# A conditioned transformer block on one core: the prologue is reordered, the first attention block runs over two key halves, and its first denominators move to TensorE

## The chip, the core and the metric

The kernel runs on one core of a Trainium2 chip. The metric is the device time of one execution in microseconds (us). A core has TensorE (PE; its weight loads are listed as PEld), VectorE (DVE), ScalarE (ACT), GpSimd (POOL) and SyncE (SP), each with its own instruction stream; they meet at semaphores. SP issues nearly all DMAs here. Matrix products go to PSUM, which has 8 banks of 512 f32 columns on 128 partitions.

## The reference

```
mod = silu(c) @ w_mod              # 1024 -> 6 x 1024: sa, ca, ga, sb, cb, gb
h = layernorm(x) * (1 + ca) + sa   # x is 2048 x 1024, bf16
q = h @ wq (32 heads of 32);  k = h @ wk;  v = h @ wv     # one k and one v for all heads
p = softmax(q k^T / sqrt(32));  a = (p v) @ wo
x = x + ga * a
h = layernorm(x) * (1 + cb) + sb
x = x + gb * ((silu(h @ w1) * (h @ w3)) @ w2)             # F = 3584
```

`ca` is called the scale part of the modulation below, and `sa` the shift part.

## The kernel before, in words

**A planner writes the order.** `Dag.add` (line 42) records every operation with its engine, the keys it reads and writes, a planned duration and a priority (a lower number goes first). `Dag.schedule` (line 106) then plays the whole program through with these durations and fixes one order per engine; `emit` writes it with semaphore waits. So an engine executes in a fixed order, and an operation that waits holds up all that stands behind it on its engine. `clear` keys make an operation wait for earlier readers and writers; `after` fixes the order of DMAs on SP. On PE score products (class S) come first, value and denominator products (V, D) next to them, and all other products are filler by priority and by order in the program. For a product group the planner also picks a free PSUM bank. Line 205 has a rule that holds a long DVE operation back while a product group is about to end; with `LOOK = 0.0` (line 13) it is off.

**Prologue (lines 455 to 761).** SP loads the 16 tiles of x (128 x 1024) into 8 slots and the first 2048 columns of `w_mod` (shift and scale together) in 8 row blocks of 512 KB, in the order of the list `ORDER` (line 645). The condition vector goes through silu to `SCT`; 128 products with one moving column each (line 677) give shift and scale. DVE makes `MODC` (1 + scale, line 687) and `SAB` (shift, line 689). Each x tile gets its statistics (`ln_stats`, line 506, on DVE; two tiles by `ln_stats_act`, line 514, on ACT), its factor on POOL (`ln_scale`, line 528), and is normalised on DVE (`ln_norm`, line 542). `ln_transpose` (line 548) transposes it on PE against the identity (line 558) and ACT (line 569) or DVE (line 572) copies it to `HT`. Scale and shift are not applied to the tiles: the scale goes into the weights (`WQ`, `WKV`: lines 719, 721 and 750), the shift into biases (products of the raw weights with `SAB`, lines 693 to 708 and 741), which are added when K (`kproj`, line 603), V (`vproj`, line 616) and Q (`qproj`, line 627) leave PSUM (lines 612, 622, 632). Then `gate` (line 768) makes `ga` and `gb` on all partitions, with weights in three slots `WMS`; `ga` is multiplied into `WO` (line 794). Lines 809 and 817 make `cb` and `sb`. The Q products of the later 1536 rows (line 824) are filler of the first attention block.

**Attention (line 830), for each of 8 blocks of 256 queries.** A block loops over 8 groups of four heads (f) and 8 steps of 256 keys. A step has 8 score products of 32 x 256 (line 855, four of them side by side on the array's row quarters) and two exponentials of 128 x 1024 on ACT (line 865), which write slot u of 11 in `UREG`. DVE adds the exponentials of four steps into a tree tile `TR` (lines 879 and 884: per group 6 additions of 128 x 2048), and line 889 folds the group's two tree tiles into one, for groups 0 to 6. Value products (line 902) take the slots as moving operand; denominator products (line 922) multiply the folded tile with a selection matrix `SEL`, one group behind. DVE copies sums to `ASB` (line 929) and denominators to `DSB` (lines 937, 940), takes reciprocals (line 946), spreads them over the partitions (`stream_shuffle` into `RB`, line 952) and multiplies (line 957).

**After a block: `post` (line 982).** Products with `WO` (line 996), the residual, the second normalisation, transposes (on PE in the first and the last block, by DMA in the others), then the gated network in 14 pairs of groups (products line 1030, tanh on ACT line 1039, line 1042 and 1047 on DVE) and the last products (line 1064). Its products are filler under the next block's attention.

Of the kernel before, what the change touches and what calls it, by code (L numbers as in the profile page):

```python
# [8 lines left out]
P = 128  # L9
# [3 lines left out]
LOOK = 0.0  # L13
# [15 lines left out]
class Dag:  # L29


    def __init__(self, nc):
# [7 lines left out]
        self.chain = 0  # L40

# [64 lines left out]
    def schedule(self, banks):  # L106
# [41 lines left out]
        while left:  # L148
# [56 lines left out]
            if e == "dve" and LOOK and n.dur > 0.9 and n.prio > 1:  # L205
                fin = None
                for b in banks:
                    g = bank_group[b]
                    rem = [x for x in g.nodes if x.start is None and x.eng == "pe"] if g is not None else []
                    if rem:  # L210
                        f1 = t_free["pe"] + sum(x.dur for x in rem) + 0.26
                        if fin is None or f1 < fin:
                            fin = f1
                if fin is not None and t < fin < t + LOOK:
                    t_free["dve"] = fin
                    continue
            ready[e].remove(n)
# [132 lines left out]
def build(nc, x_in, wq_in, wk_in, wv_in, wo_in, w1_in, w3_in, w2_in, c_in, wmod_in, out, S, D, F):  # L350
# [34 lines left out]
    BP = (0, 0, 0)  # L385
    WP = (4, 4, 4)
    RP = (0, 0, 0)
# [6 lines left out]
    RB = sb("RB", [P, QB], F32)  # L394
    WKR = sb("WKR", [P, NC, 4, 32], BF16)
    ASB = XN[:, 2:4, :].rearrange("p a d -> p (a d)").bitcast(F32).rearrange("p (a q) -> p a q", a=4)
    DSB = WKR[:].rearrange("p c a f -> p (c a f)").bitcast(F32).rearrange("p (a q) -> p a q", a=2)
# [25 lines left out]
    NR = len(RING)  # L423
    assert NF * QB + 2 * 4096 <= NC * S and NXS == 8
# [5 lines left out]
    WQ0R = WKR[:].rearrange("p c a f -> p c (a f)")  # L430
    WQ0K = ["WKR"]
# [20 lines left out]

    cuts = {}
    G.add("pool", lambda e: e.memset(SEL[:], 0.0), writes=["SEL"], dur=0.3)
    for a, fs in enumerate(DGRP):
        edge = [32 * j // len(fs) for j in range(len(fs) + 1)]
        for j, f in enumerate(fs):
# [4 lines left out]
    G.add("pool", lambda e: e.memset(IDENT[:], 0.0), writes=["IDENT"], dur=0.2)  # L462
    G.add("pool", lambda e: e.affine_select(IDENT[:], IDENT[:], pattern=[[-1, P]], compare_op=ALU.not_equal,
                                            fill=1.0, base=0, channel_multiplier=1),
          reads=["IDENT"], writes=["IDENT"], dur=0.4)

# [5 lines left out]
    def xload(t0, n):  # L472
        r = []
        for t in range(t0, t0 + n):
            r.append(dma(lambda e, t=t: e.dma_start(X[:, t % NXS, :], x2[t * P:(t + 1) * P, :]),
                         ("x", t % NXS), writes=[("X", t % NXS)], nbytes=P * D * 2))
        return r

    WQK = [("WREG", "q")]
    xload(0, 8)  # L480

    def wmload(k, after=()):
# [52 lines left out]
    def xnt(q):  # L535

        return XN[:, q, :] if q < 4 else UREG[:, (NU + NTR - 2) * 2048 + (q - 4) * D:][:, 0:D]
# [607 lines left out]
```

## Time and profile before

| | us |
|---|---|
| median of 3 runs | 1168.52 (1167.83 to 1172.24) |
| the profiled execution, its own time | 1172.46 |
| its span | 1170.7 |
| PE busy | 1124.0 (96%) |
| ACT busy | 1028.9 (88%) |
| DVE busy | 1013.7 (87%) |
| exponentials (line 865), 1024 instructions | 974.3 |
| first exponential starts | 36.41 |
| DMA, of 211 MB in all | mean 180 GB/s; 397 to 404 GB/s from 5 to 20 us |

All durations in the prediction come from this one profiled execution, so its sums are made against 1170.7 us of span, and 1172.46 of time. Idle time is charged to what ended it. "PEclk" is the granted TensorE clock, 1.00 being full speed. In rows of a timeline the first number is the start, the second the time that the row takes. In rows of a window the first number after the borders is the window's length, and each engine's busy time is followed by its number of instructions.

### The profile page before, as it was taken

Reading aid. Unit: us, or ns where it says so; the run is one execution under the profiler, and the core shown is the slowest. Engines: PE = TensorE matmul, PEld = TensorE weight load, DVE = VectorE, ACT = ScalarE, POOL = GpSimd, SP = SyncE. Lnnn points to the kernel's source line nnn. Section 1 sums busy time; section 2 is a strip of 40 time slices with the busy share of each in tenths; the row PEclk is TensorE's granted clock in tenths of the full one; section 3 lists DMA queues with packets and bytes.
Section 4 is the critical chain, followed back from the end, with each engine's and each line's share of the span. In section 5 each row is a group of like instructions: output and inputs, shape, how many; then the busy total and the mean of one; then the engine's idle time right before and its main releaser. Section 6 shows DMA issues by size and latency. Waiting matters only on the chain.

```text
span 1170.7 us, 34975 instructions
## 1 busy us (share of the span) xinstructions
PE 1124.0 (96%) x15561; PEld 757.9 (65%) x15561; DVE 1013.7 (87%) x1504; ACT 1028.9 (88%) x1174; POOL 43.1 (4%) x86
## 2 busy tenths in 40 slices
PE   4898997999989999999999999999999999999998
PEld 4554442667656676676666766767666757677887
DVE  7687988898988999899989998999989998997451
ACT  3798999899999999999999999999999999992110
POOL 5100000000010001000000001000100000000000
PEclk9897998899999999999999999999999999999999
DMA  9606007365757565966587566856596658656996
GB/s 348 216 23 196 19 2 181 109 181 160 200 129 211 169 169 133 278 182 170 156 233 204 164 179 175 246 166 174 144 257 176 191 145 246 198 161 176 299 291 154
DMA packets 383222, 211.05 MB, mean 180 GB/s; under 512 B 21600, under 2 KB 374880, under 8 KB 383072
## 3 DMA queue, kind: packets, MB, share of 16 engines
q1 hardware_dynamic: 380992, 208.69, 63.4%
q8 instruction: 122, 2.00, 0.7%
q10 hardware_dynamic: 2080, 0.13, 0.1%
q14 instruction: 28, 0.23, 0.1%
HBM read 201.46 MB, written 4.19 MB: 176 GB/s over the span
## 4 chain that ended last, share of the span: by engine, by line
PE 74%; ACT 15%; DVE 8%; issue 2%; POOL 1%; DMA 0%; SPq 0%
PE PB L1030 23%; PE PB L1064 15%; ACT UREG L865 14%; PE SP L855 11%; PE PB L902 9%; PE PB L629 4%; PE PB L996 4%; PE SP L1030 3%; DVE UREG L884 2%; PE SP L1064 2%; DVE UREG L879 1%; PE PB L922 1%; PE PB L608 1%; DVE HREG L1042 1%; PE SP L558 1%
## 5 line engine op out<-in xcount | busy, mean ns | idle before, releaser
L865 ACT ACTIVATE UREG<-SP 128x1024 bf16<-128x1024 f32 x1024 | 974.3, 1113 | 21.1 <-PE SP L855 18.8
L884 DVE TENSOR_TENSOR UREG<-UREG 128x2048 bf16<-128x2048 bf16 x256 | 311.9, 1218 | 11.6 <-ACT UREG L865 9.4
L855 PE MATMUL SP<-QT,KT 32*128 32x256 bf16 x4096 | 206.4, 276 | 16.4 <-ACT UREG L865 15.8
L1030 PE MATMUL PB<-QT,WREG 128*128 128x256 bf16 x1632 | 205.6, 273 | 0.8 <-DVE WKR L940 0.4
L1030 PEld LDWEIGHTS PB<-QT,WREG 128*128 128x128 bf16 x1632 | 148.2, 98 | 47.1 <-issue 31.7
L879 DVE TENSOR_TENSOR UREG<-UREG 128x2048 bf16<-128x2048 bf16 x128 | 156.2, 1220 | 13.2 <-ACT UREG L865 9.6
L855 PEld LDWEIGHTS SP<-QT,KT 32*128 32x128 bf16 x4096 | 61.0, 92 | 141.0 <-ACT UREG L865 91.8
L902 PE MATMUL PB<-UREG,V 128*32 128x256 bf16 x4032 | 134.1, 282 | 1.4 <-ACT UREG L865 1.4
L1030 PE MATMUL PB<-QT,HREG 128*128 128x256 bf16 x1056 | 132.9, 273 | 0.7 <-DVE WKR L940 0.4
L902 PEld LDWEIGHTS PB<-UREG,V 128*32 128x32 bf16 x4032 | 101.2, 99 | 28.4 <-issue 17.5
L1030 PEld LDWEIGHTS PB<-QT,HREG 128*128 128x128 bf16 x1056 | 96.1, 98 | 29.7 <-issue 19.7
L1064 PE MATMUL PB<-WREG,HREG 128*128 128x256 bf16 x840 | 104.9, 273 | 0.5 <-DVE HREG L1042 0.5
L1064 PEld LDWEIGHTS PB<-WREG,HREG 128*128 128x128 bf16 x840 | 77.8, 98 | 22.2 <-issue 12.6
L1030 PE MATMUL PB<-QT,X 128*128 128x256 bf16 x544 | 69.1, 273 | 1.1 <-DVE WREG L1037 0.7
L629 PE MATMUL PB<-HREG,WREG 128*128 128x512 bf16 (+1 forms) x312 | 67.8, 355 | 1.8 <-ACT HREG L569 0.9
L889 DVE TENSOR_TENSOR UREG<-UREG 128x2048 bf16<-128x2048 bf16 x56 | 68.2, 1218 | 0.4
L1064 PE MATMUL PB<-HREG 128*128 128x256 bf16 x532 | 67.1, 273 | 0.0
L1039 ACT ACTIVATE GSB<-GSB 128x512 bf16<-128x512 bf16 x56 | 41.6, 742 | 28.1 <-DVE GSB L1037 28.1
L929 DVE COPY XN<-PB 128x256 f32<-128x256 f32 x63 | 26.6, 422 | 39.8 <-PE PB L922 38.0
L1039 ACT ACTIVATE WREG<-WREG 128x512 bf16<-128x512 bf16 x56 | 42.8, 765 | 20.1 <-DVE WREG L1037 20.1
L1030 PEld LDWEIGHTS PB<-QT,X 128*128 128x128 bf16 x544 | 49.8, 98 | 15.9 <-issue 10.7
L996 PE MATMUL PB<-WO,QT 128*128 128x512 bf16 x232 | 57.8, 381 | 0.4 <-DVE WREG L1070 0.4
(130 smaller groups left out, 1004.2 us busy)
## 6 DMA issues: line engine op xcount, KB each, us to landing
WREG<-in_B_w_dram SPq DMA_DIRECT2D x112, 512.0 KB, 5.1
HREG<-in_B_w_dram SPq DMA_DIRECT2D x74, 512.0 KB, 5.4
WREG<-in_B_w_dram SPq DMA_DIRECT2D x33, 896.0 KB, 5.2
X<-in_B_w_dram SPq DMA_DIRECT2D x38, 512.0 KB, 5.0
HREG<-in_B_w_dram SPq DMA_DIRECT2D x21, 896.0 KB, 5.3
X<-in_B_w_dram SPq DMA_DIRECT2D x10, 896.0 KB, 5.0
X<-in_A_x_dram SPq DMA_DIRECT2D x32, 256.0 KB, 5.6
WREG<-in_w_mod_dram SPq DMA_DIRECT2D x16, 512.0 KB, 5.2
```

What stands on the lines that cost most here:

```text
L629: g = mm_group(NC, lambda e, b, c: e.matmul(b[:, 0:n], WQ[:, c, f * P:(f + 1) * P], HT[:, c, sl], start=c == 0, stop=c == NC - 1), lambda ...
L855: r = e.matmul(SP[:, b, o:o + qn], KT[32 * gg:32 * gg + 32, kts[j] * P:(kts[j] + 1) * P], QT[32 * gg:32 * gg + 32, f, q0:q0 + qn], start=T ...
L865: G.add("act", lambda e, u=u, h0=h0, n=n, b0=b0, nb=nb: e.activation(U[:, u, h0 * W:(h0 + n) * W].rearrange("p (b w) -> p b w", b=nb), SP[ ...
L879: G.add("dve", lambda e, tr=tr, u=u, fu=first_u: e.tensor_tensor(TR[:, tr, 0:4 * W], U[:, fu, 0:4 * W], U[:, u, 0:4 * W], ALU.add), reads= ...
L884: G.add("dve", lambda e, tr=tr, u=u: e.tensor_tensor(TR[:, tr, 0:4 * W], TR[:, tr, 0:4 * W], U[:, u, 0:4 * W], ALU.add), reads=[("TR", tr) ...
L889: G.add("dve", lambda e, ta=ta, tb=tb: e.tensor_tensor(TR[:, ta, 0:4 * W], TR[:, ta, 0:4 * W], TR[:, tb, 0:4 * W], ALU.add), reads=[("TR", ...
L902: r = e.matmul(PB[g.bank][32 * gg:32 * gg + 32, 0:qn], V[:, kt, :], U[:, pu, (gg * npk + j) * qn:(gg * npk + j + 1) * qn], start=w0 + n == ...
L929: G.add("dve", lambda e, g=g, f=f: e.tensor_copy(ASB[:, f % 4, 0:qn], PB[g.bank][:, 0:qn]), writes=[("ASB", f % 4), ("XN", 2 + f % 4 // 2) ...
L996: g = mm_group(NC, lambda e, b, f, t=t, h=h: e.matmul(b, QT[:, f, t * P:(t + 1) * P], WO[:, f, h * 512:(h + 1) * 512], start=f == 0, stop= ...
L1030: return e.matmul(b[:, j * qn:(j + 1) * qn], w13[:, w, c, j * P:(j + 1) * P], QT[:, c, q0:q0 + qn], start=c == 0, stop=c == NC - 1)
L1039: G.add("act", lambda e, b=b: e.activation(TB[b], GS[b], ACT.Tanh, scale=0.5), reads=[("GS", b)], writes=[("TB", b)], clear=alias("TB") if ...
L1064: G.add("pe", lambda e, g=g, j=j, fc=fc, hf=hf, first=first, w2s=w2s: e.matmul(PB[g.bank][:, j * 256:(j + 1) * 256], HHT[:, hf * NH + fc, ...
```

## The change

Seven things, in the order of the program:

1. **The planner's hold on DVE** is rewritten and switched on. A DVE operation planned at over 0.9 us (tree sums and folds) is put off if an operation of priority -1 or less is ready within 0.5 us, or, if neither of PSUM banks 0 and 1 is idle or about to be, until the next product group ends, when that is within 0.6 us. It acts in all blocks.
2. **Dummy products** of 128 x 128 identity on PE can be planned into idle time up to `WARM`; with `WARM = 0.0` none are made.
3. **Loads.** The modulation is loaded in halves of 256 KB per row block: the scale half (`a`) of all rows is in front of the shift half (`s`). The raw `wq` goes to `WO`'s place in three cuts (group 0, groups 1 to 3, groups 4 to 7), and `wo` is loaded there once their readers are done.
4. **Scaling into new places.** Scaled K and V weights get their own tile `WKS`; scaled Q weights go from `WO` to `WQ`, so that products no longer wait for the bias products to have read the raw ones. Scaling of groups 1 to 3 is shared between ACT and DVE, that of groups 4 to 7 has the last priority on DVE. Biases come in three sets, each with its Q cut.
5. **Transposes.** All 16 normalised tiles get places of their own. A transpose group waits for all its tiles. Tiles 0 to 7 are evicted by ACT, tiles 8 to 15 by DVE.
6. **The first attention block** is split: groups 0 to 3 (`HEAD`) first run over keys 0 to 1023, then over keys 1024 to 2047, then groups 4 to 7 run as before. For the halves of groups 0 to 3 there are no tree sums: `DIRECT` has PE sum the exponentials themselves with `SEL`. The second half's sums are added to the first's in `ASB`.
7. **Priorities after the first block**: `BP` and `RP` become 5 for it (normalisation, transposes and division ahead of the rest of DVE). `RB` moves into the tile of normalised rows, with four slots in the first block: all spreads first, then all products.

The core of the diff:

```diff
-LOOK = 0.0
+LOOK = 0.5
+LK = 0.6
+LF = 0.5
+UP = -1
...
-            if e == "dve" and LOOK and n.dur > 0.9 and n.prio > 1:
...
+            if e == "dve" and n.dur > 0.9 and n.prio > UP:
+                soon = [c for c in cands if c[1].prio <= UP and c[0] < t + LOOK]
+                if soon:
+                    t_free[e] = min(c[0] for c in soon)
+                    continue
+                fin = t + LK
+                for b in (0, 1):
+                    i = bank_idle(b)
+                    if i is not None and i <= t + LF:
+                        fin = None
+                        break
...
-    BP = (0, 0, 0)
+    BP = (5, 0, 0)
...
-    RP = (0, 0, 0)
+    RP = (5, 0, 0)
+    RBQ = (0,)
...
+    WARM = 0.0
+    HEAD = 4
+    DIRECT = (0, 1)
...
-                G.add("pe", tr, reads=[("XN", q0 + i), "IDENT"] + xnk(q0 + i), dur=ncb * 0.065, lat=0.2,
+                G.add("pe", tr, reads=["IDENT"] + [k for j in (range(nt) if i == 0 else (i,)) for k in [("XN", q0 + j)] + xnk(q0 + j)], dur=ncb * 0.065, lat=0.2,
...
-    ONACT = (3, 6)
...
-    ORDER = ("w0", "w1", "w2", "w3", "x8", "x9", "w4", "x10", "x11", "w5", "w6", "w7", "q", "x12", "x13", "x14", "x15")
...
+    ONACT = (2, 5)
...
+    QACT = 1
+    TRP = 1
+    EV = (("act",), ("act",), ("dve",), ("dve",))
+    ORDER = ("x0", "x1", "x2", "x3", "x4", "x5", "a0", "a1", "x6", "a2", "a3", "x7", "a4", "a5", "a6", "a7", "q0",
+             "s0", "s1", "s2", "s3", "s4", "s5", "s6", "s7", "q1", "x8", "x9", "x10", "x11", "x12", "x13", "x14", "x15", "q2")
+    QCUT = (0, 1, HEAD, NC)
...
+    gm = [grp((0,)), grp((1,))]
+    for h in (1, 0):
+        for k in range(NC):
...
+    def wscale(a, keys):
+        G.add("dve", lambda e: e.tensor_tensor(WKS[:, a], WKV[:, a], bc1(32), ALU.mult), reads=[("MODC", 1)] + keys,
+              writes=[("WKS", a)], dur=dve_t(256), prio=-5 if a == 0 else 1)
...
+            if k == 1 and c % 2 < QACT:
+                G.add("act", lambda e, c=c: e.activation(WQ[:, c, a:b], WO[:, c, a:b], ACT.Identity, scale=MODC[:, 1, c:c + 1]),
+                      reads=[("MODC", 1), ("WQR", k)], writes=wr, dur=act_t(b - a), prio=1)
...
+    bias(0, (0,), kb=True)
+    G.chain = 0
+    kproj(0, 256, (2, 3, 4, 5, 6, 7))
+    qproj(0, 256, 0, (2, 3, 4, 5, 6, 7), prio=1)
+    kproj(256, 256, (2, 3, 4, 5, 6, 7))
+    kproj(512, 512, (1,))
+    wscale(1, WVK)
+    qscale(1)
+    bias(1, (0,), vb=True)
+    qproj(0, 256, 1, (0, 1))
+    vproj(0, (0, 1))
+    vproj(1, (0, 1))
+    for f in range(2, HEAD):
+        qproj(0, 256, f, (0, 1))
+    tr(8, 4, (0, 1))
...
+    bias(2, (0, 1))
+    G.chain = 0
+    qscale(2)
     wo_load = dma(lambda e: e.dma_start(WO[:], wo_in.rearrange("(c p) f -> p c f", p=P)), "wo", writes=["WO"],
...
+                  clear=[("WQR", k) for k in range(3)], nbytes=D * D * 2, after=xl)
...
+            direct = q0 == 0 and f < HEAD and s // per_t in DIRECT
...
+            if direct:
+                ds.append((f, pend, h))
+                dprev[0] = None
...
+                            a = U[:, a[0]] if us else TR[:, a]
...
+            if h == 1:
+                G.add("dve", lambda e, g=g, f=f: e.tensor_tensor(ASB[:, f % 4, 0:qn], ASB[:, f % 4, 0:qn], PB[g.bank][:, 0:qn], ALU.add),
...
+        if q0 == 0:
+            head = []
+            for h in range(2):
+                for f in range(HEAD):
+                    head += [(f, s) for s in range(h * per_t, (h + 1) * per_t)] + [(f, (h,))]
+            sched = head + [x for x in sched if x[0] >= HEAD]
...
+    G.warm = (WARM, P / 2400.0 + 0.0026, warm, ident)
```

## The prediction

> **What bounds the kernel now.** I read the page's busy slices first, to see which engines are full and when.
>
> ```profile
> PE   4898997999989999999999999999999999999998
> ACT  3798999899999999999999999999999999992110
> PEclk9897998899999999999999999999999999999999
> ```
>
> One slice is 29.3 us. PE and ACT are both full from the third slice on; the gaps are at the start, in slices 5 to 8, and on ACT at the end. Next I cut the span at every 128th exponential (128 exponentials are one block of 256 queries) and read busy time and clock per stretch. The columns are PE, weight load, DVE, ACT, POOL, granted clock, DMA.
>
> ```profile
> 0.00:36.40 36.40, 20.87 (x361) 17.43 (x365) 29.03 (x71) 14.72 (x26) 16.19 (x48) 1.00 1.00 353
> ...
> 36.40:171.50 135.10, 126.91 (x1773) 63.11 (x1767) 109.85 (x157) 124.46 (x136) 2.20 (x6) 0.91 0.25 79
> 171.50:300.00 128.50, 114.83 (x1642) 73.16 (x1635) 114.51 (x163) 123.15 (x141) 2.49 (x4) 0.93 0.55 152
> ...
> 426.13:552.26 126.13, 125.87 (x1803) 85.64 (x1801) 117.49 (x171) 125.47 (x143) 3.44 (x4) 1.00 0.69 190
> ```
>
> The repeating block takes 126.13 us with PE busy 125.87 and ACT 125.47: a new prologue has nothing to win there. What can be won lies in three stretches: the 36.4 us before the first exponential, block 0 (135.1), block 1 (128.5). The rest, 1170.7 - 300.0 = 870.7 us, I keep. On ACT, block 0 shows a hole:
>
> ```profile
> 45.76 2.37 ACT L569 ACTIVATE HREG<-PB 128x512 bf16<-128x512 bf16 x4
> 48.01 1.03 ACT L865 ACTIVATE UREG<-SP 128x1024 bf16<-128x1024 f32 x1
> 48.92 2.09 ACT L569 ACTIVATE HREG<-PB 128x512 bf16<-128x512 bf16 x4
> 50.83 1.09 ACT L865 ACTIVATE UREG<-SP 128x1024 bf16<-128x1024 f32 x1
> 56.38 3.77 ACT L865 ACTIVATE UREG<-SP 128x1024 bf16<-128x1024 f32 x4 [4.46 <-PE SP L855]
> ```
>
> From 45.8 to 56.4 ACT does two exponentials. It evicts the last 8 transposed pieces (4.5 us) and then waits 4.46 us for scores, because keys 1536 to 2047 are late. Last, the DVE timeline from modulation to first scores:
>
> ```profile
> 26.02 0.11 DVE L687 TENSOR_SCALAR MODC<-PB 128x8 f32<-128x8 f32 x1
> ...
> 26.24 1.22 DVE L721 TENSOR_TENSOR WREG<-WKR,MODC 128x1024 bf16<-128x1024 bf16 x1
> ...
> 29.69 0.15 DVE L711 COPY BIA<-PB 128x2 f32<-128x2 f32 x1
> ...
> 34.86 0.48 DVE L632 TENSOR_SCALAR QT<-SP,BIA 128x256 bf16<-128x256 f32 x1 [0.53 <-PE SP L629]
> ```
>
> The modulation is there at 26.1, yet the first exponential runs at 36.41. These 10.3 us hold the weight scaling, the bias copy behind normalisations on DVE, a K product (1.90 us) and a Q product, with transposes between.
>
> **Start: 36.4 becomes 25.5.** The new order loads 8 x tiles, 8 scale halves, the first Q columns, then 8 shift halves. Scale and shift are each 2.1 MB. Bytes against time come from the modulation products of before: the fourth weight row (4.3 MB with x) was there at 15.1 us, and the fifth (5.4 MB) at 17.7, after a DMA wait. So scale is complete near 15.1. Shift is complete at 6.7 MB, 1.3 MB past 17.7 us, at 340 to 400 GB/s: 21.0 to 21.6, I take 21.3. Now K and Q products no longer wait for shift; only their evictions do, through the bias. So the chain after 21.3 is: last modulation product and semaphores 0.5, SAB copy 0.4, bias products for Q and K 0.8 (their rows now are 0.40 and 0.38), copy 0.3, KT and QT evictions 0.48 each, scores to exponential 0.6: 3.6 us, plus 0.6 for a DVE instruction in the way. That is 25.5. Scale first thus does not start anything by itself: the shift part ends the wait as before, but 6 us of other work has moved ahead of it. Bounds: 24 with DVE free, 30 if the chain stretches to 8 us, near its present 10.3.
>
> The SP queue issues all of this without a wait (26 issues of about 0.45 us, row median of w_mod, done by 12.5 us), and tile 8 is the first that waits for a slot. The Q columns in 256 KB took 9.9 us to land at the end of the queue; now they delay shift by their bytes, counted above. The two small POOL fills of IDENT move ahead of SEL: nothing waits for SEL until the denominators.
>
> **Block 0: 135.1 becomes 128.** Four query groups run over keys 0 to 1023 first: 4 x 8 = 32 exponentials at 0.92 us (20 in 18.45 us in the chain) give 29 us of work, from 25.5 to about 55, before the second key half is wanted. Its x tiles land by about 28 and need 8 x 2.1 us of DVE (two statistics 1.28, aggregate 0.20, normalise 0.55) and 16 evictions of 0.41, 23 us together; DVE has room because the tree sums of these groups are gone. So the hole closes: 4.46 us of wait off. The 8 evictions leave ACT: 4.4 off. Scaling Q weights on ACT adds 4 x 0.45 = 1.8. That gives 135.1 - 4.5 - 4.4 + 1.8 = 128.0.
>
> DIRECT sums denominators on PE: per group 64 column tiles in each of two halves against 8 after the fold, a row of 4 tiles taking 0.116 us (64 in 1.86). Per half 8 rows of 4, so 64 rows for 4 groups, less 8: 56 x 0.116 = 6.5 us more PE. It saves DVE 4 x 7 x 1.22 = 34.2 us, and adds 8 evictions, 3.4 us. DVE was busy 109.85 of 135.1, so its saving alone is worth nothing after about 60 us. PE is where it tells: 126.9 + 6.5 = 133.4 us does not fit into 128. What makes room is the clock: it was 0.91 on the mean, and 0.50 from 44.5 to 55, in the hole, where about 9 us busy cost 4.5 too many. That leaves 128.9, about the 128 taken; what is over runs in block 1, where PE was idle 13.7 us. The other 6 us of ACT stalls of block 0 (80 to 120 us, at half clock) I leave as they are.
>
> **Block 1: 128.5 becomes 127.** BP and RP put the first block's normalisation and transposes ahead of the tree sums on DVE. Now PE waits twice for a normalised tile there, 2.8 us in all, and ACT falls behind by some 3. I take half, 1.5; bounds 0 to 3.
>
> **Costed at nothing.** A transpose group waits for all its tiles: PE used to wait inside the group, so the same wait stands earlier (bounds -1 to +1). Scaling the rear Q columns has the last DVE priority and holds the WO load; behind it on SP stand gate weights and post(0) tiles. First use of WO was at 186 us, WO landed at 39: 50 us or more of cover, at full price if DVE leaves it until 100. RB now lies in the normalisation tile: its first write of a block comes a third of the block after the last read. The hold on long DVE sums (LOOK, LK) reaches all blocks; see the third rival.
>
> **A rule against it.** PE stays lightly loaded until 25 us, and nothing warms it (WARM is 0). These rows are PE's:
>
> ```profile
> 18.81 3.62 PE L558 MATMUL SP<-IDENT,UREG 128*128 128x128 bf16 x32 [0.47 <-DVE UREG L544]
> ...
> 34.10 0.61 PE L558 MATMUL SP<-IDENT,XN 128*128 128x128 bf16 x8
> ```
>
> A transpose costs 0.113 us at 18.8 and 0.076 at 34.1, although the granted clock reads 1.00 in both places. The Trainium skill, "TensorE: Matmul & The Clock Gate", Part 1, says that an idle array runs at half clock until a window of some 3.4 us has been busy; the trace agrees, PE being dense from 30.0 and fast by 34, so the clock column misses the cold start. Its section "Why this matters for your kernels" asks for no gaps over some 3 us. By the rule, score, K and Q products in the first 10 us after 25.5 could all run at half speed, 5 us lost; by the row, dense work warms PE within 4 us, some 2 lost. I take the row: new PE work there (K, V, Q products, transposes, direct sums) is about 37 us in 30, so PE is dense.
>
> **Sum.** 25.5 + 128 + 127 + 870.7 = 1151.2 us of span against 1170.7: 19.5 less. The profiled run took 1172.46, 1.8 above its span and 3.9 above the median 1168.52. From the median: 1168.5 - 19.5 = 1149.0 us.
>
> **Rivals.** First, PE is the bound and its clock no better: block 0 keeps 133.4 busy and its 8.2 us idle, 141.6; with 25.5 and 127 the sum is 1164.8, 5.9 less, 1162.6. For it: PE is 100% busy from 125 to 173. Against: the half clock lies in the hole that goes. Second, PE stays dense, the clock losses of block 0 and 1 (some 12 and 8 us) mostly go and ACT runs through: block 0 at its 117.8 + 1.8 = 119.6, block 1 at 125: 1140.8, that is 1138.6. Against: PE is short of work while gate weights arrive.
>
> Third, slower: the hold delays long DVE sums everywhere. A repeating block has 56 of them (1.22 us) and 126.13 - 117.49 = 8.6 us of DVE slack. The slack is gone at 8.6/56 = 0.15 us of mean hold; the gain of 19.5 over 7 blocks is 2.8 more per block, so from 11.4/56 = 0.20 us the kernel is slower. At 0.3 us: 16.8 - 8.6 = 8.2 per block, 57 in all, 1206. For it: no PE wait on DVE in the repeating block could pay for it. Against: the hold falls away when either PSUM bank is idle.
>
> **Chances.** What such a kernel's times can tell from no change is about 0.5%, 5.8 us. Main forecast, 1140 to 1158: 0.62; first rival and what lies between, 1158 to 1163: 0.19, and its part within 0.5%: 0.07; second rival, below 1140: 0.07; third: 0.05. Faster 0.88, same 0.07, slower 0.05. The range 1135 to 1162 leaves out the third rival and the ends of the first two.
>
> **What would show it.** First exponential at 24 to 30 us; no gap over 1 us on ACT between it and 60 us; the 256th near 280 us; clock 1.00 from 35 to 60; block of 126.1 us after. I am wrong if the shift bias comes late on DVE, if PE stays at 0.50 through the first key half, or if the repeating block changes.

## The result and the profile after

The changed kernel took 1161.39 us (median of 4 runs, 1160.08 to 1162.85) against 1170.38 for the kernel before on the same chip (4 runs, 1167.83 to 1172.74): ratio 0.9924, 95% interval 0.9895 to 0.9953. It is faster by 9.0 us, or 7.1 against the median of 1168.52 that the forecast started from. The forecast was 19.5. The profiled execution took 1161.32 us with a span of 1159.5, so it is a typical one.

The slices of the page, one being 29.0 us, answer to those shown of before:

```profile
PE   5799998999979999999999999999999999999998
ACT  5789998999999999999999999999999999992110
PEclk9899998999989999999999999999999999999999
```

ScalarE (ACT) starts earlier, 5 against 3 in slice 1, but it has gained nothing in slices 2 and 3: 7 and 8, against 7 and 9 before. The low place of TensorE (PE) in slice 7 has risen from 7 to 8. The gaps of the first block are still there. The spans are cut again at every 128th exponential. The columns are the window, its length, then busy time (and count) of PE, weight load, VectorE (DVE), ACT, POOL, and the granted clock, DMA share and GB/s.

```profile
0.00:29.13 29.13, 16.50 (x317) 13.82 (x317) 16.98 (x43) 16.57 (x31) 12.36 (x38) 1.00 0.99 333
29.13:162.30 133.17, 124.00 (x2020) 67.88 (x2017) 95.62 (x175) 120.92 (x128) 6.65 (x16) 0.97 0.33 104
162.30:291.80 129.50, 124.79 (x1739) 79.88 (x1737) 119.69 (x176) 125.96 (x143) 3.29 (x4) 0.97 0.62 168
415.30:541.40 126.10, 125.69 (x1803) 85.74 (x1801) 117.03 (x171) 125.59 (x144) 3.43 (x4) 1.00 0.68 189
1048.10:1159.50 111.40, 107.01 (x1021) 92.53 (x1019) 54.04 (x96) 11.96 (x20) 1.69 (x4) 1.00 0.90 233
```

The last row is the tail behind the last exponential. By stages, read from the starts of the 1st, 129th, 257th and 385th exponential in each profile:

| us | before | forecast | after | difference |
|---|---|---|---|---|
| first exponential | 36.4 | 25.5 | 29.1 | -7.3 |
| block 0 | 135.4 | 128.0 | 133.2 | -2.1 |
| block 1 | 130.9 | | 129.5 | -1.5 |
| block 2 | 126.7 | | 126.6 | -0.1 |
| from the 385th to the end | 741.3 | | 741.1 | -0.2 |

(The cuts of before in the prediction lay up to 3 us from these starts; its block 1 was 128.5 there and was forecast at 127. The 29.1 is one profile's: four kernels below, with the higher Q priority, with the hold off, with both and with the direct sums cut down, have the same order on PE up to 40 us and start at 28.1 to 29.7.) So the start gave two thirds of the 10.9 us that were forecast, block 0 less than a third of the 7.1 us, and the rest is as forecast. ACT's timeline shows where block 0 loses; each row is a stretch without a gap, with the idle time ahead of it and its releaser in brackets.

```profile
29.13 1.94 ACT L925 ACTIVATE UREG<-SP 128x1024 bf16<-128x1024 f32 x2 [0.88 <-PE SP L915]
31.68 1.94 ACT L925 ACTIVATE UREG<-SP 128x1024 bf16<-128x1024 f32 x2 [0.61 <-PE SP L915]
34.40 7.44 ACT L925 ACTIVATE UREG<-SP 128x1024 bf16<-128x1024 f32 x8 [0.78 <-PE SP L915]
42.60 1.94 ACT L925 ACTIVATE UREG<-SP 128x1024 bf16<-128x1024 f32 x2 [0.76 <-PE SP L915]
46.62 9.27 ACT L925 ACTIVATE UREG<-SP 128x1024 bf16<-128x1024 f32 x10 [2.08 <-PE SP L915]
61.45 11.46 ACT L925 ACTIVATE UREG<-SP 128x1024 bf16<-128x1024 f32 x12 [5.56 <-PE SP L915]
```

The hole is still there: 5.56 us ahead of 61.45, after 24 exponentials that took 32.3 us instead of the 22 that their 0.92 us each would need. All gaps are ended by score products (line 915), so PE is late each time. Ahead of the last of these products PE works without a gap:

```profile
56.54 1.05 PE L1002 MATMUL PB<-UREG,SEL 128*32 128x256 bf16 x32
57.41 1.05 PE L975 MATMUL PB<-UREG,V 128*32 128x256 bf16 x32
58.28 1.05 PE L1002 MATMUL PB<-UREG,SEL 128*32 128x256 bf16 x32
59.26 1.05 PE L658 MATMUL PB<-HREG,WREG 128*128 128x256 bf16 x8
...
61.00 0.40 PE L915 MATMUL SP<-QT,KT 32*128 32x256 bf16 x8
```

These are direct sums (line 1002), value products (line 975) and the Q product of group 3 (line 658). From 29.13 to 61.45 as a whole PE was busy 26.4 of 32.3 us; 4.1 us of its waits there were for exponentials. From 61.45 to the 65th exponential at 100.11 it was busy 38.2 of 38.7.

**The start.** DVE's timeline of the changed kernel:

```profile
17.10 0.15 DVE L722 TENSOR_SCALAR MODC<-PB 128x8 f32<-128x8 f32 x1
...
24.92 0.17 DVE L748 CAST SAB<-PB 128x8 bf16<-128x8 f32 x1 [4.75 <-PE PB L713]
26.74 0.16 DVE L778 COPY BIA<-PB 128x1 f32<-128x1 f32 x1 [1.66 <-PE PB L771]
```

The scale part came at 17.10, early as planned, and DVE then waited 4.75 us for the shift part. For the line that loads `w_mod` the profile has (duration of an issue on SP in ns, then issue to landing)

```profile
L695 SPq DMA_DIRECT2D UREG<-in_w_mod_dram x16: 432/432/2117, 4.0 to 15.0; - x16
...
DMA to landing us min/median/max: 5.3/6.3/8.0
```

The last issue was at 15.0 and landed 8.0 us later, so the last shift row was there at 23.0 and not at 21.3. One issue took 2.117 us instead of 0.43: the one right behind the load of the first Q columns, which has rows of 256 bytes. It looks like the culprit, but the row that it issued was not late:

```profile
L695 SPq DMA_DIRECT2D UREG<-in_w_mod_dram x1: 2117/2117/2117, 9.8 to 9.8; - x1
...
DMA to landing us min/median/max: 7.4/7.4/7.4
```

It landed at 17.27. The Q columns, issued at 9.37, had landed at 16.59, so the row came 0.68 us behind them, the usual distance of two such rows: the long issue delayed no landing. By the landing times the 1.7 us are three things. The scale half was complete at 15.5 instead of 15.1. The Q columns took 1.12 us of the queue, where as many bytes of `w_mod` take 0.68. And the seventh shift row came 1.57 us behind the sixth (22.20 behind 20.63) instead of 0.68. From 19 to 21 us, just ahead of this, the DMA list has one packet on the instruction queue:

```profile
q8 instruction: 1, 0.02, 3.3%
```

(3.3% of 16 DMA engines in 2 us is one engine for about 1.06 us.) In each of the 14 profiles one row lands 0.8 to 1.5 us late, 2.2 to 3.0 us after such a packet starts; with the dummy products below the packet came at 15.5, and the late row was the one at 18.45. That the packet is the cause is inferred from this; no run tests it. The kernel before has it as well, behind the row at 17.7 us from which the prediction reckons on. The next row of `w_mod` there is this:

```profile
L483 SPq DMA_DIRECT2D UREG<-in_w_mod_dram x1: 433/433/433, 13.7 to 13.7; - x1
...
DMA to landing us min/median/max: 7.6/7.6/7.6
```

So 1.05 MB past the row at 17.7 were there only at 21.2, and 1.57 MB at 22.6. For the 1.3 MB of the prediction this makes about 21.9 (an estimate between the two), not 21.3.

PE did not use the last row at once either:

```profile
23.42 0.40 PE L713 MATMUL PB<-SCT,UREG 128*128 128x1 bf16 x8
23.68 1.01 PE L587 MATMUL SP<-IDENT,UREG 128*128 128x128 bf16 x8
24.48 0.40 PE L713 MATMUL PB<-SCT,UREG 128*128 128x1 bf16 x8
...
25.05 1.01 PE L637 MATMUL SP<-HREG,WKS 128*32 128x256 bf16 x16
```

The order puts eight transposes between two shift products here, and they take 1.01 us, where they take 0.61 on a fast array (first experiment). From one shift product to the next PE needs 1.06 us, and rows land 0.68 us apart, so PE falls behind; with the array fast it needs 0.65 (in the kernel with late Q columns, below). The last product ran at 24.48, 1.5 us behind its row.

### The profile page after: what moved, and what is told of

It is laid out like the page before. It is cut to its first block, busy times and chain, and to the rows that moved or that the text cites. A ratio compares the mean times of both kernels' runs of the same rounds, so it can differ in the third digit from the quotient of the medians.

```text
span 1159.5 us, 35436 instructions
## 1 busy us (share of the span) xinstructions
PE 1117.8 (96%) x15785; PEld 760.2 (66%) x15785; DVE 984.9 (85%) x1498; ACT 1027.8 (89%) x1170; POOL 44.6 (4%) x86
## 4 chain that ended last, share of the span: by engine, by line
PE 92%; DVE 3%; ACT 3%; POOL 1%; DMA 0%; issue 0%; SPq 0%; DVEq 0%
PE PB L1141 33%; PE PB L1175 16%; PE SP L915 14%; PE PB L975 11%; PE PB L1107 5%; PE PB L658 4%; PE SP L1141 3%; ACT UREG L925 3%; PE SP L1175 2%; PE PB L1002 2%; DVE ST L530 1%; PE PB L637 1%; PE PB L838 0%; PE SP L1107 0%; DVE WO L850 0%; DMA X<-in_A_x_dram 0%
## 5 line engine op out<-in xcount | busy, mean ns | idle before, releaser
L948 DVE TENSOR_TENSOR UREG<-UREG 128x2048 bf16<-128x2048 bf16 x240 | 292.8, 1220 | 12.8 <-ACT UREG L925 10.8
L915 PE MATMUL SP<-QT,KT 32*128 32x256 bf16 x4096 | 205.6, 275 | 16.7 <-ACT UREG L925 16.5
L942 DVE TENSOR_TENSOR UREG<-UREG 128x2048 bf16<-128x2048 bf16 x120 | 146.4, 1220 | 11.5 <-PE PB L1002 6.4
L975 PEld LDWEIGHTS PB<-UREG,V 128*32 128x32 bf16 x4032 | 99.1, 98 | 28.3 <-issue 18.1
L1141 PEld LDWEIGHTS PB<-QT,HREG 128*128 128x128 bf16 x1056 | 96.1, 98 | 29.7 <-issue 19.7
L1175 PE MATMUL PB<-WREG,HREG 128*128 128x256 bf16 x812 | 101.1, 273 | 0.0
L1175 PEld LDWEIGHTS PB<-WREG,HREG 128*128 128x128 bf16 x812 | 75.4, 98 | 20.4 <-issue 11.4
L658 PE MATMUL PB<-HREG,WREG 128*128 128x512 bf16 (+1 forms) x312 | 64.1, 342 | 0.3 <-DVE DSB L1026 0.3
L957 DVE TENSOR_TENSOR UREG<-UREG 128x2048 bf16<-128x2048 bf16 x52 | 63.4, 1220 | 0.5
L1150 ACT ACTIVATE GSB<-GSB 128x512 bf16<-128x512 bf16 x56 | 38.7, 692 | 27.4 <-DVE GSB L1148 27.4
L1175 PEld LDWEIGHTS PB<-HREG 128*128 128x128 bf16 x532 | 49.3, 98 | 14.3 <-issue 8.0
L551 POOL TENSOR_SCALAR RS<-MV 128x1 f32<-128x1 f32 x32 | 19.3, 608 | 1018.1 <-DVE MV L532 1017.8
```

Source lines behind the costliest of these rows:

```text
L658: g = mm_group(NC, lambda e, b, c: e.matmul(b[:, 0:n], WQ[:, c, f * P:(f + 1) * P], HT[:, c, sl], start=c == 0, stop=c == NC - 1), lambda ...
L915: r = e.matmul(SP[:, b, o:o + qn], KT[32 * gg:32 * gg + 32, kts[j] * P:(kts[j] + 1) * P], QT[32 * gg:32 * gg + 32, f, q0:q0 + qn], start=T ...
L942: G.add("dve", lambda e, tr=tr, u=u, fu=first_u: e.tensor_tensor(TR[:, tr, 0:4 * W], U[:, fu, 0:4 * W], U[:, u, 0:4 * W], ALU.add), reads= ...
L948: G.add("dve", lambda e, tr=tr, u=u: e.tensor_tensor(TR[:, tr, 0:4 * W], TR[:, tr, 0:4 * W], U[:, u, 0:4 * W], ALU.add), reads=[("TR", tr) ...
L957: G.add("dve", lambda e, ta=ta, tb=tb: e.tensor_tensor(TR[:, ta, 0:4 * W], TR[:, ta, 0:4 * W], TR[:, tb, 0:4 * W], ALU.add), reads=[("TR", ...
L975: r = e.matmul(PB[g.bank][32 * gg:32 * gg + 32, 0:qn], V[:, kt, :], U[:, pu, (gg * npk + j) * qn:(gg * npk + j + 1) * qn], start=w0 + n == ...
```

## The experiments

My theory for the start: the shift half came late because the Q load in front of it held up the issues, and PE's half speed delayed its product. For block 0: PE has too much work there, so a stall that is closed comes back later (theory L). The rivals: the order of a few instructions is at fault and can be mended; or the execution of before that the forecast was made against was itself not typical.

The kernels ran on several chips, and each ratio is to the kernel before on the same chip. Near 0.99 the intervals of two kernels overlap, so the readings rest on the stages of the profiles.

### Dummy products up to 26 us

```diff
-    WARM = 0.0
+    WARM = 26.0
```

> The changed kernel with WARM at 26: 114 dummy products of 128x128 fill the planned gaps on PE up to 26 us. Reference numbers of the changed kernel: SAB copy at 24.9 us, first exponential at 29.1, 8 transposes in 1.01 us, span 1159.5. Theory A (the cold clock on PE delays the shift products, which stand among transposes): the transposes fall to about 0.6 us for 8, SAB at 22 to 23, first exponential at 26 to 27, time down 2 to 3 us. Rival B (the shift half lands late): SAB and first exponential stay within 0.5 us, time the same. Rival C: dummies stand before needed work in PE's fixed order and push it back, first exponential later than 29.1.

Measured: 1160.55 us (4 runs), ratio 0.9927 (0.9904 to 0.9951), no gain over the changed kernel. PE's timeline of this kernel:

```profile
15.03 0.61 PE L587 MATMUL SP<-IDENT,XN 128*128 128x128 bf16 x8
...
21.42 1.01 PE L587 MATMUL SP<-IDENT,UREG 128*128 128x128 bf16 x8
...
24.36 0.40 PE L713 MATMUL PB<-SCT,UREG 128*128 128x1 bf16 x8
```

The dummies did their work on the first transposes, eight in 0.61 us, but PE had two gaps of about 0.5 us between 17 and 19, one for the scale part and one for the late shift row, and by 21.4 it was slow again. The last shift product moved from 24.48 to 24.36 and the first exponential from 29.1 to 29.4. So the warmth did not last through the wait. That the gaps ended it is not shown: with the Q columns loaded late (below) PE waited 0.72 us ahead of 19.48 and stayed fast.

### Transposes of tiles 4 to 7 behind the last shift product

```diff
-                G.add("pe", tr, reads=["IDENT"] + [k for j in ...
+                G.add("pe", tr, reads=["IDENT"] + list(xr) + [k for j in ...
...
-                     EV[t0 // 4], allow=allow, prio=TRP)
+                     EV[t0 // 4], allow=allow, prio=TRP, xr=["SHD"] if t0 == 4 else [])
...
+                  writes=["SHD"] if h == 0 and k == NC - 1 else [],
```

> The changed kernel, but the transposes of tiles 4 to 7 are put behind the last shift product in PE's order. Theory A (order and cold clock on PE, data there by about 21.3 us): SAB copy at 22 instead of 24.9 us, first exponential at 26 to 27 instead of 29.1; part of it is given back at the third and fourth exponential pair, since keys 256 to 1023 come later. Rival B (the shift half lands at about 24): SAB stays at 24 to 25.

Measured: 1164.99 us (6 runs), ratio 0.9958 (0.9940 to 0.9976). The last shift product still ran at 24.51, the first exponential came at 31.7, and the hole was 7.24 us. PE's timeline of this kernel shows why:

```profile
22.38 1.01 PE L658 MATMUL SP<-HREG,WREG 128*128 128x256 bf16 x4
...
23.44 0.80 PE L658 MATMUL SP<-HREG,WREG 128*128 128x256 bf16 x3
...
24.51 0.37 PE L713 MATMUL PB<-SCT,UREG 128*128 128x1 bf16 x8
```

The planner fills the places with Q and K products, which run at half speed too (four of 128 x 256 in 1.01 us; eight took 1.05 at 26.71 in the changed kernel). So it is not the transposes as such: this other filler in front of the last shift product costs the same, and the transposes, moved behind it, make keys late.

### First Q columns loaded behind the shift half

```diff
-    ORDER = (... "a6", "a7", "q0", "s0", ... "s7", "q1", ...)
+    ORDER = (... "a6", "a7", "s0", ... "s7", "q0", "q1", ...)
```

> The changed kernel with the first Q columns (256 KB in rows of 256 bytes) loaded behind the shift half instead of ahead of it. In the changed kernel the issue of the first shift row right behind it took 2.1 us on SP instead of 0.43, and the last shift row landed at 23.0 us. Theory (that transfer holds up SP's issue and with it the shift half): the last shift row lands at 21.0 to 21.5, SAB copy at 23 to 23.5 instead of 24.9; the Q columns then land at 23 to 25, and the first exponential moves by -1.5 to +1 from 29.1. Rival (the DMA engines' throughput alone sets it): the last shift row lands at 22.4 or later, only the bytes of one transfer earlier.

Measured: 1157.23 us (4 runs), ratio 0.9886 (0.9862 to 0.9911). The load of `w_mod` and PE's timeline in this kernel, as above:

```profile
L695 SPq DMA_DIRECT2D UREG<-in_w_mod_dram x16: 432/432/686, 4.0 to 12.8; - x16
...
DMA to landing us min/median/max: 5.5/6.7/9.3
```

```profile
21.33 0.61 PE L587 MATMUL SP<-IDENT,UREG 128*128 128x128 bf16 x8
21.77 0.34 PE L713 MATMUL PB<-SCT,UREG 128*128 128x1 bf16 x8
...
22.62 0.35 PE L713 MATMUL PB<-SCT,UREG 128*128 128x1 bf16 x8
```

The last shift row was issued 2.2 us earlier, but it landed at 22.1, only 0.9 us earlier. So the long issue had not held it up: what went were the 1.12 us of the Q columns in the queue, less 0.2 by which the late row was later. Of theory (21.0 to 21.5) and rival (22.4 or later) the rival is nearer. The last shift product gained more, from 24.48 to 22.62, because PE ran it 0.5 us behind its row and no longer 1.5: the array was fast here at 21 us. The first exponential came at 27.6, 1.5 earlier than in the changed kernel and 0.5 earlier than in any of the same order, and block 0 took 129.4 (3.9 less). Why the array was fast is not shown, and neither is why block 0 gained more than the start did. This profile has the array at full speed from 40 to 46 us, where that of the changed kernel has it at half. But with the dummies it was at 0.72 there, and block 0 still took 132.9.

### Q products of groups 1 to 3 at higher priority

In the changed kernel the hole ended with the Q product of group 3, at 59.26.

```diff
-    qproj(0, 256, 1, (0, 1))
+    qproj(0, 256, 1, (0, 1), prio=1)
...
-        qproj(0, 256, f, (0, 1))
+        qproj(0, 256, f, (0, 1), prio=1)
```

> The changed kernel with the Q products of groups 1 to 3 (first 256 queries) at priority 1, so that PE takes them ahead of value and direct denominator products. Theory D (the 5.6 us hole on ACT at 56 us is one of order: the group 3 Q product stands behind four value and denominator groups): no wait of ACT over 2 us between 46 and 62, block 0 shorter by 4 to 6 us, time down 3 to 6. Rival E (PE has too much work there, whatever the order): the hole moves to a later place of block 0 and block 0 stays within 2 us of 133.2.

Measured: 1166.17 us (9 runs), ratio 0.9968 (0.9954 to 0.9983). ACT's timeline of this kernel:

```profile
54.68 7.44 ACT L925 ACTIVATE UREG<-SP 128x1024 bf16<-128x1024 f32 x8 [1.35 <-PE PB L1002]
64.06 1.94 ACT L925 ACTIVATE UREG<-SP 128x1024 bf16<-128x1024 f32 x2 [1.93 <-PE PB L1002]
...
70.55 1.94 ACT L925 ACTIVATE UREG<-SP 128x1024 bf16<-128x1024 f32 x2 [2.47 <-PE SP L915]
```

The hole closed: the 25th exponential came at 56.5 instead of 61.5. But now exponentials wait for slots that the direct sums (line 1002) still have to read, and by the 65th the 5 us were down to 0.4 (99.7 against 100.1). Block 0 took 135.7. So this order alone does not mend it: PE has the same work to do ahead of the 65th exponential, and the wait comes back there. The time also grew by 4 us in the rest (745.4 against 741.1), which is taken up below.

### Trees instead of direct sums in the first block

```diff
-    DIRECT = (0, 1)
+    DIRECT = ()
```

> The changed kernel with DIRECT empty: the two key halves stay, but DVE adds the exponentials of groups 0 to 3 in tree tiles and PE sums only those. PE has 56 rows of four column tiles less, about 6.5 us by the sum of the prediction; DVE has 24 additions of 1.22 us more, 29 us, beside the normalisation of tiles 8 to 15. If PE's load is what keeps block 0 at 133.2: block 0 down by 3 to 6 us. If DVE's room was needed for the second key half: tiles 12 to 15 are late, hole of over 6 us on ACT near 55, block 0 at 136 or more.

Measured: 1165.1 us (6 runs), ratio 0.9958 (0.9941 to 0.9974). ACT stood still for 10.60 us before 59.22, and block 0 took 139.7. DVE, with its tree sums back, gets to the normalisation of the second key half later: to the last tile at 56.95 instead of 50.17. The direct sums earn 6.5 us of block 0 on this account, although they load PE; 3.0 of them come back in block 1 (126.5 against 129.5).

### No key halves and no direct sums

```diff
-    DIRECT = (0, 1)
+    DIRECT = ()
...
-        if q0 == 0:
+        if q0 < 0:
             head = []
```

> The changed kernel without the two key halves and without direct sums: the first block's groups run over all 2048 keys one after another, with tree sums, behind the new prologue. It separates the prologue's part from the halves' part. If the halves are what fills ACT while keys 1024 to 2047 are made: only 8 exponentials by about 40 us, then a hole of some 15 us until about 55 (tree variant with halves had one of 10.6), block 0 at 140 or more, so that the early start is wholly given back and time is at 1168 or above. If the halves are worth little because PE is the bound: block 0 within 3 us of 133.3.

Measured: 1190.53 us (4 runs), ratio 1.0170 (1.0142 to 1.0199). After eight exponentials ACT waited 19.22 us, until 58.67, and block 0 took 151.6; 12 us more were lost in the tail (taken up below). An earlier start without the halves and the direct sums is worse than the kernel before: the halves are what fills ACT.

### Three quarters of the direct sums left out, same order

```diff
-                    for x in range(len(td) * npk):
+                    for x in range(2 if us else len(td) * npk):
...
```

> The changed kernel with the same order on every engine, but the denominator sums of the eight key halves take only the first of their four steps (8 products instead of 32 each; three quarters of these denominators are left out of the computation). That takes 24 x 0.033 = 0.79 us of TensorE from each half, 6.3 us in all at full clock and twice that at half. Theory L (TensorE's load is what keeps ScalarE waiting in block 0): the stalls between 40 and 62 us shrink, the 25th exponential comes at 57 to 59 instead of 61.5, block 0 falls from 133.3 to 127 to 129 and the time to 1155 to 1157. Theory O (order and late operands, not load): the 25th exponential stays within 1 us of 61.5, block 0 at 132 or more, time 1159 to 1162, and TensorE idles more. A third outcome, that a lighter TensorE loses more to the half clock, would show as a longer block 0 with clock under 0.95.

Measured: 1157.55 us (6 runs), ratio 0.9890 (0.9870 to 0.9911), and in ACT's timeline

```profile
44.70 9.27 ACT L925 ACTIVATE UREG<-SP 128x1024 bf16<-128x1024 f32 x10 [0.86 <-PE SP L915]
58.30 17.84 ACT L925 ACTIVATE UREG<-SP 128x1024 bf16<-128x1024 f32 x19 [4.33 <-PE SP L915]
```

The stall before the ten exponentials fell from 2.08 to 0.86 us, the hole from 5.56 to 4.33, and the 25th exponential came at 58.3, as theory L expected, though 0.8 us of its gain is an earlier start (28.3) that this edit cannot have made. Block 0 took 129.7: 3.5 us less for 6.3 us of PE work (at full clock) taken out, a little short of the 4.3 to 6.3 that it had expected. The clock is not the reason: over block 0 it was 0.96 on the mean here and 0.97 in the changed kernel. Chance may be some of it: the hold-off kernel below, of the same order up to the 65th exponential, took 132.1. So 6.3 us of PE work less make 2.4 to 3.5 us of block 0: PE's load is a good part of the cause. That the order of keys, values and Q products holds the remaining hole is argued from PE's idle time ahead of it.

### The kernel before with the new priorities alone

```diff
-    BP = (0, 0, 0)
+    BP = (5, 0, 0)
...
-    RP = (0, 0, 0)
+    RP = (5, 0, 0)
```

> The kernel before with one part of the change alone: BP and RP at 5 for the first block, so that its normalisation, transposes and division come ahead of tree sums on DVE. Prediction: the first exponential (36.4) and block 0 (135.4) as before, block 1 down by 1.5 us (0 to 3) from 130.9, time down by as much. Rival: nothing, since the wait there is the chain from the last division over POOL, not DVE's queue.

Measured: 1168.37 us (20 runs), ratio 0.9999 (0.9987 to 1.0011): nothing. This kernel has the same order as before on PE, ACT, POOL and SP, and one pair of instructions exchanged on DVE. Yet its profiled block 0 took 132.1 us and that of before 135.4. PE's windows, of before and of this kernel:

```profile
110.00:120.00 10.00, 9.96 (x142) 0.70 0.31 92
```

```profile
110.00:120.00 10.00, 8.70 (x136) 1.00 0.35 107
```

The same stretch had a mean clock of 0.70 in one and 1.00 in the other. Single runs of the kernel before spread from 1167.0 to 1173.3 us (29 of them beside this one); the profiled one at 1172.46 lay near the top. The exchanged pair is not the cause of the 3.2 us between them: it runs at 175 to 180 us, behind block 0, and up to there every engine has the same order. So they are chance. Against a block 0 of 132.1 the changed kernel's 133.2 is no gain at all, and what is left of the change is mostly the earlier start.

### The hold off

```diff
-            if e == "dve" and n.dur > 0.9 and n.prio > UP:
+            if e == "dve" and n.dur > 99 and n.prio > UP:
```

> The changed kernel with the planner's hold on long DVE operations off in all blocks. Theory (the hold is worth nothing where PE and ACT are full): repeating block 126.1 us as with it, time within 2 us of the changed kernel (1161.4). Rival F (the hold costs DVE room in every block): repeating block shorter by 0.3 us or more, time down by 2 or more. Rival G (the hold is what keeps PE supplied with banks in block 0 and 1): block 0 or block 1 longer by 2 us or more.

Measured: 1174.64 us (10 runs), ratio 1.0048 (1.0035 to 1.0061): without the hold the change makes the kernel slower. The start of the 1024th exponential is not later, 1045.7 against 1048.1. What is longer is the tail behind it, in PE's windows:

```profile
1045.70:1173.50 127.80, 123.34 (x1170) 0.99 0.89 236
```

That is 127.8 us instead of 111.4, with 1170 products instead of 1021. In the instruction order of PE itself, 595 first products of the gated network (line 1141) stand behind the last score product, and 450 in the changed kernel. A row of 144 of them in the tail takes 16.4 us, so 145 more are 16.5 us: the whole difference. In each block before, PE idled 1.2 to 2.8 us more (busy 122.8 to 124.4 of 126 us from 418 to 922 us, against 125.6), and the attention ran on without its filler. The same count explains two earlier runs: 482 with the higher Q priority (tail 115.3) and 555 without the halves (tail 123.2).

### The hold alone on the kernel before, and no hold with another order

```diff
-LOOK = 0.0
+LOOK = 0.5
+LK = 0.6
+LF = 0.5
+UP = -1
...
+                soon = [c for c in cands if c[1].prio <= UP and c[0] < t + LOOK]
...
```

> The kernel before with the hold on long DVE operations alone (the new rule and its four constants), nothing else. In the hold-off version of the changed kernel the exponentials end as early as with it, but 595 gated-network products instead of 450 are left behind the last score product on TensorE, and the tail takes 127.8 us instead of 111.4. Theory P (the hold matters only through the order that the planner falls into: what counts is how many products it leaves for the tail): before has 450 left, with the hold also 450, so its blocks stay at 126.1 us, the tail at 111.6 and the time within 3 us of 1168. Theory H (the hold itself frees TensorE in each block): the rest from the 385th exponential falls by up to 14 us, to 727, time near 1155.

Measured: 1169.76 us (14 runs), ratio 0.9995 (0.9982 to 1.0008): the hold alone does nothing to the kernel before. The second kernel has the hold off and the higher Q priority, both edits shown above:

> The changed kernel with the hold off and the Q products of groups 1 to 3 at priority 1. Its order leaves 450 products for the tail, where hold-off alone left 595 and the same Q priority with the hold left 482. Theory P (order's tail): the tail is 111 to 112 us without any hold, the rest from the 385th exponential 741, time near 1162 (Q priority with hold had 1166.2, of which 4 us were its 32 products more in the tail). Theory H (the hold itself is needed): the rest stays near 755 and the time is 1174 to 1176. The hole on ScalarE near 56 us should be closed as with the Q priority before, and given back by the 65th exponential.

Measured: 1160.6 us (6 runs), ratio 0.9911 (0.9891 to 0.9930). The rest is 741.3 us, and the tail, all engines in the columns of the first table,

```profile
1046.70:1158.30 111.60, 107.16 (x1023) 92.67 (x1020) 54.32 (x96) 12.13 (x20) 1.70 (x4) 1.00 0.88 233
```

is that of the changed kernel without any hold. So the hold has no worth of its own. What counts is the order that the planner falls into: if the repeating blocks keep PE supplied (448 of these products in each), 450 are left at the end; if not, products pile up for the tail. Whether it falls into the good order hangs on small things: the hold, a priority, the halves.

### What helped, together

First Q columns behind the shift half, dummies until 26 us, the higher Q priority, and the hold off (450 products left with this order).

> What helped so far put together: first Q columns loaded behind the shift half (1157.2), dummy products until 26 us (1.5 us at the 385th exponential), Q products of groups 1 to 3 at priority 1 (0.7 us there), and the hold off, which with this order leaves 450 products for the tail. If the gains add up: first exponential near 27.7, 385th near 411.5, tail 111.4, time near 1155. If the hold itself is needed (theory H): rest near 755, time near 1169. If the gains do not add: 1157.

Measured: 1154.02 us (4 runs, 1152.74 to 1154.69), ratio 0.9855 (0.9832 to 0.9877), the best of all. Its first exponential comes at 28.7, the 385th at 411.2, and ACT's timeline has

```profile
45.52 14.77 ACT L925 ACTIVATE UREG<-SP 128x1024 bf16<-128x1024 f32 x16 [0.48 <-PE SP L915]
```

where the changed kernel had its hole: 16 exponentials without a gap. Its median is 7.4 us below that of the changed kernel, on another chip; the two ratios to before are 0.9855 and 0.9924, and their intervals do not overlap. With the late Q columns alone (0.9886) they do; by the profiles this kernel is 2.5 us ahead of that one at the 385th exponential. The dummies did nothing for the start, which is 1.1 us later than with the late Q columns alone.

## Why the prediction was wrong, and what held

From profile to profile the forecast missed by 8.4 us: by 3.6 at the start and by 5.0 in block 0, with 0.2 won back later. The other 2.1 us of the miss in the medians are the execution that it was made against.

**"Shift is complete at 6.7 MB ... I take 21.3": sized too small by 1.7 us.** The step took its rate from the stretch up to 17.7 us. It left out that the Q columns, in rows of 256 bytes, take 1.12 us and not 0.68, and it left out one late row, which its own profile shows behind 17.7. The row landed at 23.0. The long issue of 2.1 us, by which SP was done with these rows at 15.4 and not at 12.5, has no part in it.

**"Last modulation product and semaphores 0.5": short by 1.5.** The term has no wait on PE. The product ran at 24.48, behind transposes at half speed (in the second experiment behind K and Q products, at 24.51). From the product to the first exponential it took 4.65 us, against 4.2 in the forecast for landing to exponential. So 1.7 + 1.5 + 0.45 make up the 3.6 us by which 29.1 misses 25.5.

**The rule and the row.** The prediction let a row of before (fast after 4 us of dense work) decide, on the ground that "PE is dense", over the Trainium skill's "TensorE: Matmul & The Clock Gate", whose section "Why this matters for your kernels" asks for no idle gaps over some 3 us. Neither figure held. PE was dense from 19.69, but 16 K products still took 1.01 us at 25.05; eight Q products in 1.05 us, twice as fast as in the second experiment, came at 26.71, 7 us after the dense stretch began. Then it idled again, in gaps of at most 1.32 us, well under the skill's 3, as PE's windows (length, busy, granted clock, DMA share, GB/s) show:

```profile
34.00:40.00 6.00, 3.62 (x108) 0.96 0.18 46
40.00:46.00 6.00, 6.00 (x105) 0.50 0.45 137
46.00:52.00 6.00, 4.23 (x74) 0.97 0.02 5
```

After 6 us at 3.62 busy it ran the next 6 at 0.50, so 3 us of work at full speed took 6. Those 3 us and the slow stretch at 20 to 26 us are nearer to the 5 us that the prediction worked out by the rule than to the 2 by the row.

**"So the hole closes: 4.46 us of wait off": failed.** What comes late next is PE, not x tiles or DVE. The terms on ACT were nearly right: its busy time went from 124.5 to 120.9, by 3.6 us against the -4.4 + 1.8 = -2.6 of the sum. Its idle time went from 10.6 to 12.3 instead of to about 6.1. That the new Q priority only moves the wait, and that block 0 gets shorter (by about 3.5 us) when PE work is taken out, is shown; the rest of the hole stays open.

**"What makes room is the clock": mis-sized.** The term was 4.5 us of clock loss in the hole of one profiled execution. The clock did rise, from 0.91 to 0.97 on the mean, but it lost 3 us in a new place. And the execution that the forecast was made against lay 3.9 us above the median, with 3.2 us more in block 0 than the profile of a kernel with the same order there. I used its stage lengths as if they were typical, and subtracted the whole from the median. (The 6.5 us of more PE work stand: the 64 column tiles named there are those of both halves together, and the sum takes 8 rows of 4 per half.)

**What held.** Block 1: forecast -1.5, profile -1.5, by luck: the priorities alone gave nothing. PE was busy 7.5 us longer in it than before (124.8 against 117.3 by the same cuts), where the working had left 0.9 us over for it. The rest: 741.3 to 741.1. But the ground for that, that the hold could win nothing there since before's PE hardly waits, missed the point: in the changed kernel with its old Q priority, no hold would have cost some 13 us. The third rival had the sign of the hold wrong.

**The first rival** gave 1162.6, and 1161.4 was measured. Its mechanism, that PE is the bound in block 0, is the one that the runs support, in part. Its number is partly luck: it kept the early start at 25.5 and put block 0 at 141.6 with PE busy 133.4; measured were 29.1, 133.2 and 124.0.

## What to carry to other kernels

Cost a wait on data not only by the bytes ahead of it but by the later landings that the profile of before already shows, and by what stands in front of its first user on the engine, at that engine's speed of the moment. A long issue is not yet a late landing: compare the landing times. Before stage lengths of one execution go into a sum, ask how far that execution lies from the median. When a stall closes, ask whether the engine that ended it has spare time in the following 40 us; if not, the stall moves. In a kernel whose order comes from a greedy planner, count what is left behind the last step of the main loop: 145 products more or less there outweighed the whole rebuilt prologue.

## What was not expected of the hardware

Behind a DMA of 256 KB with rows of 256 bytes the next issue on the same queue took 2.1 us instead of 0.43 (3.9 us with the late Q columns, where the next one had rows of 768 bytes), and yet no landing waited for it. A packet on the instruction queue is followed by a row that lands 0.8 to 1.5 us late, in every profile here. PE gave eight transposes in 0.61 us after transposes and one-column products only (late Q columns, at 20.03), so dense work of these two kinds alone was enough there. Whether the array is fast at this place differs between profiles of the same order: in the hold-off kernel eight transposes took 0.61 us at 20.84 and 1.01 at 22.05, with a granted clock of 0.50 from 22 to 24 us; in the changed kernel they took 1.01 all along, with a clock that reads 1.00. And two executions with the same order differed by 3.2 us in one block of 135, at 0.70 and 1.00 of clock in the same 10 us.
